# A new table of order, engines and banks for the same 2788 pieces of work, in an attention and gated-MLP kernel on one core

## The chip, the cores and the metric

One core of a Trainium2 chip runs the whole program. The metric is device time in microseconds (us) of one execution. TensorE is PE in the rows (its weight loads PEld), VectorE DVE, ScalarE ACT, GpSimd POOL. SyncE (SP) issues the transfers.

## What is computed

Attention with a multiplicative decay, then a gated projection. For each of 8 batches and 8 heads, with 576 positions and 64 dimensions a head:

```python
scores = q @ k.T / sqrt(64) + (cum[:, None] - cum[None, :])   # cum = cumsum(log(clip(f, 1e-4, 1)))
attn   = softmax(causal(scores)) ; attn_out = attn @ v
x      = attn_out with the heads side by side                  # (8, 576, 512)
gate   = sigmoid(causal depthwise conv of 5 taps over x)
out    = (gate * (x @ w_val)) @ w_out                           # float32
```

## The kernel before

**Pieces.** The two heads of a batch that share 128 partitions are a *pair*; there are 32. The kernel never writes its instructions in program order. It first records 2788 pieces of work (`Plan.add`, `Plan.dma`, lines 139 to 165), each with the buffers that it reads and writes, the engines that could run it, and the PSUM banks that it is the first to touch. Then it walks a table.

- *Loads* (`load_pair`, `load_rest`, lines 306 to 322): the pair's q and k go into `Xr[i % 2]`, its values into `vt[i % 2]`. The decay rows go into `dm[...]` and `dl[i % 2]` by broadcast from a DRAM tensor `decd`, which the kernel makes itself at the start.
- *Splits* (`plan_t`): from pair 4 on, `Xr` is split into a rounded part `Xh` (line 278) and a rest `Xl` (line 392), so that three fast matmuls replace a float32 one. Pairs 0 to 3 use `Xr` as it is.
- *Scores* (`plan_s`, lines 400 to 488): three PE groups a pair (line 263). For each of the 9 row blocks of a pair DVE adds the decay and takes the row minimum of the scaled negative (line 474), and ACT takes the exponential into `P` or `Pl` (line 478). A decay block is masked in place before its next, smaller use (`sel`), on POOL (line 483) or DVE (line 485). Pairs 0 and 1 take their decays from PE (`gate,gate` in the rows) and a fixed mask.
- *Transposes* (`plan_pt`): P is transposed by PE (lines 514, 532, 533) and copied from PSUM to `pt`, `pl` (line 278), on ACT or DVE. The reciprocals of the row sums ride along. They are written to DRAM (`rzd<-pl`) and read back by broadcast (`x<-rzd`).
- *Values* (`plan_pv`): P times V on PE, times the reciprocal (line 581), split into `xh`, `xl` (lines 278, 588). The convolution is five passes over `gate` (lines 283, 285, 623), then tanh (line 594).
- *MLP* (`plan_moe`): for each batch, the product with w_val (16 half groups, `Mv`), times the gate (line 655), split into `hh`, `hl` (line 669), and the product with w_out (`Mo`). Odd and even batches share output tiles. Results go by `ot` (lines 696, 698) to DRAM.
- *Weights* (`plan_w`): each quarter of the two weights is loaded into `ot` or `wu` and taken apart by seven short passes (lines 712 to 749).
- *Warming groups* (`warm`, line 358): six groups of four transposes of the identity, whose results nobody reads.

**What sets the order.** `TABLE` (line 46) is a string. Each entry names a piece (two digits in base 64), an engine (one digit: PE, ACT, DVE, POOL, SP) and, for each bank that the piece is the first to touch, the bank. The kernel issues the pieces in the table's order, so the table alone fixes every engine's queue. An engine takes its instructions in that order. A piece that waits holds up everything behind it on its engine, on SP too.

```python
while at < len(table):
    n, e = DIGITS.index(table[at]) * 64 + DIGITS.index(table[at + 1]), ENGINES[int(table[at + 2])]
    nd = self.nodes[n]
    at += 3
    assert nd["deps"] <= seen and e in nd["engs"]
    for k in nd["take"]:
        self.home[k] = range(int(table[at]), int(table[at]) + self.width[k])
        at += 1
    seen.update((n, done.get(n, n)))
    yield nd["fn"], e
```

Of the kernel before, what the change touches and what calls it, by code (L numbers as in the profile page):

```python
# [51 lines left out]
4p24t14z23B003N41o24v33I17k44q13z075k44E34w24x14F24G13o23m23p24A13R45V044L033A13W011p33C13U025z31s13r11t23P44B31B44C24D15W28K41u23s24K24M13q31v27x14X0
708I44T034e43X25X15w35s45v064513V27m44Y24Z41w17y34_47z17w31x21y25I0204U14V031A33t25A25x25F35511z11E20o078C44P073-
15C35G23Y15B15_041D15y15M34Q14N065D25E17A21F24O14W15J35144R075347_055N27C34S158035K25L156075S38R13u21G25P35T27o45Q29U45H13v25O11H18E4802a045928P38Q35R
15U15725Y281167028S28O3ba46017F33Z23_26813w16107690136a16b41I26219h059i26d47B002347G27D27I27J26j14037L35a19j163015Z078G47H10l055c36h46f45-
164165067M24126617K17P37E185057O0277Q29-47S37T26m018X37V37R14227U1a717Y3bg4a837W27N17u47X18U35b27Z29Y48627-
19W46k0687038816n28304a516l28226o11J284189008a15d2bi46p38T057328f0618g18j48h48b048p18c18Y28V29136w005e28-
38n48W18d068e19226x09l019315f28_26z058l48Z11M45g29839m1a62a43901953940469926A01L39626q16r21X49b39719e3az019c2aa36s2bc48s078t29a18q039d16t39f2dl4431bm3
aA29r048r29n07bp19g16P06aB11O19s26u29o16B29t049u19k26y2bn11R2ad39v039w1be46C16D36Q01K1a9047218M49x0539y16H006I09z49H1bo2ab2ae2ac1af1ag31P2bv2dr4ah2ai1
aj36E056F0bq3ak26J21Q26G2aq31S1an3al1am0431T2aD07ao2at39B4ar29p05aw3bR011U25h16K26L3aE11V1as16M001W2ap19q1dt4ax2ay1bS2bT19F4bs36N0dx2dy3aJ05aK26v1au2a  # L60
v16O2dz39D46R29I07dp49J26S16T3br03152bt21Z1bE006dA1bw2bu1by3eD42029K07bB3bx1dn4aH03aI1bV04bz28w39L2aL01bW1bC2aM16X036Y0bF38x2bG2bA1aC26U056V0bI3bJ2bO3
bH11-2eJ4eL4bL2bM2a24bD1dB3bK16Z2bP2aP014aQ1aT4bN1dD3bQ16W2aR4dG21_26-
28y2aN02aO1aZ1eH4aF07aG16_3e004e127006211222232e21aV4dC03017dE2dJ3dF1dH2dP052241dM3aX4dI1252eQ1dK2a-
04eS3b003dN2dT3fV4bU2dU2e400b12eF49M1eY3a_2dL1bk4710e51721g14734dQ29O1eR3c300dR2c41c5034cf1b42c61c74dW3dS18u17a01g81c94dZ37b08z2bX06b228A2b52bZ00dX2b6
# [763 lines left out]
```

## Time and profile before

| | us |
|---|---|
| three runs | 513.71, 515.65, 515.92 (median 515.65) |
| the profiled execution | 514.39 |
| its span, first to last instruction | 512.7 |
| PE busy | 498.9 (97%) |
| DVE busy | 434.4 (85%) |
| ACT busy | 359.8 (70%) |
| POOL busy | 230.0 (45%) |

The profiled execution lies 1.26 us under the median, and 1.7 us of it lie outside the span. PE is busy nearly throughout. What a new order can change is the time in which PE waits, so the rows to look for are PE's idle time by stretch, who ended it, and how full the engines are that feed PE in each stretch. The granted clock is 1.00 in all stretches, the higher of its two levels (2.4 GHz).

### The profile page before, as it was taken

The page shows a single profiled execution, that of the slowest core. Times are in us where ns is not written, and L with a number is a line of the kernel's source. Part 1 is how long each engine was busy: PE and PEld are TensorE (multiplying, and loading weights), DVE is VectorE, ACT ScalarE, POOL GpSimd, SP SyncE. Part 2 cuts the span into 40 slices and gives each one's busy share as a digit, 9 for nine tenths or more (in the row PEclk, how much of TensorE's full clock was granted, in tenths as well). Part 3 has the DMA queues.
Part 4 walks back from the last instruction along what each step waited for, and adds up shares of the span by engine and source line. Part 5 has one row for each costly group of instructions (what it writes and reads, how often), then busy time and mean ns, then how long its engine had stood idle before and what let it go on. Part 6 is the DMA issues. An engine that isn't in the chain of part 4 may idle for free.

```text
span 512.7 us, 12687 instructions
## 1 busy us (share of the span) xinstructions
PE 498.9 (97%) x4392; PEld 442.9 (86%) x4392; DVE 434.4 (85%) x1171; ACT 359.8 (70%) x973; POOL 230.0 (45%) x345
## 2 busy tenths in 40 slices
PE   6899899999999999999999999999999999999997
PEld 4677798988998889988999888899899888999985
DVE  6999999998988897899988988988988888977660
ACT  4999998885866765768777677787877766473122
POOL 3348785745644443347544635434742623201200
PEclk9999999999999999999999999999999999999999
DMA  7977564555563465446517364554665153122012
GB/s 264 270 232 251 174 164 158 150 164 181 169 213 102 138 182 174 153 143 195 172 58 254 104 215 129 192 183 143 203 201 176 58 156 106 45 74 68 21 63 102
DMA packets 35009, 79.49 MB, mean 155 GB/s; under 512 B 5057, under 2 KB 5313, under 8 KB 34945
## 3 DMA queue, kind: packets, MB, share of 16 engines
q1 hardware_dynamic: 34864, 78.54, 48.8%
q8 instruction: 34, 0.56, 0.5%
q14 instruction: 31, 0.25, 0.2%
q10 hardware_dynamic: 80, 0.15, 0.1%
HBM read 68.93 MB, written 9.73 MB: 153 GB/s over the span
## 4 chain that ended last, share of the span: by engine, by line
PE 77%; ACT 6%; DMA 6%; DVE 5%; issue 3%; SPq 2%; POOL 1%; DVEq 0%; ACTq 0%; POOLq 0%
PE banks L263 62%; PE banks L514 12%; ACT P L478 3%; DMA Xr<-in_x_dram 3%; PE banks L532 2%; SPq L289 2%; DVE gate L623 1%; ACT pt L278 1%; DVE banks L474 1%; DMA ot<-in_w_val_dram 1%; DMA x<-rzd 1%; PE banks L533 1%; DMA dl<-decd 1%; DMA dm<-decd 1%; ACT Xh L278 0%
## 5 line engine op out<-in xcount | busy, mean ns | idle before, releaser
L478 ACT ACTIVATE P<-banks,negm 128x512 f32<-128x512 f32 (+3 forms) x256 | 135.0, 535 | 35.2 <-DVE negm L474 33.2
L483 POOL TENSOR_SCALAR_AFFINE_SELECT dm<-dm 128x128 f32<-128x128 f32 x182 | 74.7, 420 | 122.8 <-DVE negm L474 113.0
L474 DVE CUSTOM_DVE_ANT_0 banks<-banks,dm 128x512 f32<-128x512 f32 (+3 forms) x240 | 115.1, 504 | 14.6 <-POOL dm L483 4.7
L278 ACT COPY pt<-banks 128x512 f32<-128x512 f32 (+1 forms) x185 | 93.8, 542 | 37.2 <-PE banks L514 32.2
L263 PE MATMUL banks<-xh,wall 128*128 128x288 f32 x512 | 113.4, 300 | 0.1
L623 DVE SCALAR_TENSOR_TENSOR gate<-x,cw,gate 128x576 f32<-128x576 f32 x126 | 110.2, 881 | 3.4 <-POOL gate L285 2.3
L263 PE MATMUL banks<-pt,vt 128*64 128x128 f32 (+1 forms) x1280 | 92.8, 297 | 0.4 <-DVE pt L278 0.2
L514 PE MATMUL banks<-ident,P 128*128 128x128 f32 x640 | 89.6, 277 | 2.3 <-ACT P L478 1.8
L263 PE MATMUL banks<-wall,hh 128*128 128x512 f32 x288 | 91.5, 399 | 0.0
L263 PEld LDWEIGHTS banks<-xh,wall 128*128 128x128 f32 x512 | 85.0, 188 | 1.0 <-DVE h L655 0.3
L263 PEld LDWEIGHTS banks<-pt,vt 128*64 128x64 f32 x1280 | 75.5, 137 | 8.5 <-issue 2.5
L514 PEld LDWEIGHTS banks<-ident,P 128*128 128x128 f32 x640 | 71.4, 140 | 12.3 <-ACT P L478 3.1
L263 PE MATMUL banks<-xl,wall 128*128 128x288 f32 x256 | 75.4, 295 | 0.0
L392 POOL TENSOR_TENSOR Xl<-Xr,Xh 128x640 fp32r<-128x640 f32 (+1 forms) x37 | 57.6, 1559 | 28.7 <-ACT Xh L278 12.1
L263 PEld LDWEIGHTS banks<-wall,hh 128*128 128x128 f32 x288 | 51.5, 188 | 9.0
L263 PE MATMUL banks<-Xh 128*128 128x288 f32 (+4 forms) x280 | 56.8, 335 | 0.9 <-DVE pt L278 0.5
L263 PE MATMUL banks<-wall,hl 128*128 128x512 f32 x144 | 56.5, 392 | 0.0
L478 ACT ACTIVATION_READ_ACCUMULATOR P<-banks,negm 128x1 f32 x256 | 53.2, 208 | 0.0
L263 PE MATMUL banks<-Xh,Xl 128*128 128x288 f32 (+4 forms) x280 | 53.1, 315 | 0.0
L263 PE MATMUL banks<-Xl,Xh 128*128 128x288 f32 (+4 forms) x280 | 53.0, 314 | 0.0
L263 PEld LDWEIGHTS banks<-xl,wall 128*128 128x128 f32 x256 | 48.2, 188 | 0.3
L263 PEld LDWEIGHTS banks<-Xh 64*128 64x128 f32 (+1 forms) x280 | 32.0, 185 | 10.0 <-issue 4.2
(104 smaller groups left out, 754.3 us busy)
## 6 DMA issues: line engine op xcount, KB each, us to landing
Xr<-in_x_dram SPq DMA_DIRECT2D x32, 608.0 KB
dm<-decd SPq DMA_DIRECT2D x60, 256.0 KB
vt<-in_v_dram SPq DMA_DIRECT2D x32, 320.0 KB
x<-rzd SPq DMA_DIRECT2D x64, 144.0 KB
out_dram<-ot SPq DMA_DIRECT2D x36, 256.0 KB
dl<-decd SPq DMA_DIRECT2D x60, 144.0 KB
ot<-in_w_val_dram SPq DMA_DIRECT2D x2, 512.0 KB
wu<-in_w_val_dram SPq DMA_DIRECT2D x2, 512.0 KB
```

What stands on the lines that cost most here:

```text
L263: nc.tensor.matmul(out, lhsT=lhsT, rhs=rhs, start=start, stop=stop)
L278: (eng.copy if eng is nc.scalar else eng.tensor_copy)(out=out, in_=in_)
L289: lambda e: (nc.sync if e == "SP" else nc.scalar).dma_start(out=out, in_=in_), reads, writes, **kw)
L392: eng.tensor_tensor(out=Xl[r][:, a:e], in0=Xr[r][:, a:e], in1=Xh[r][:, a:e].bitcast(F32), op=ALU.subtract)
L474: nc.vector.tensor_tensor_reduce(out=sl, in0=sl, in1=add, op0=ALU.add, op1=ALU.min, scale=-0.125, scalar=3.0e38, accum_out=negm[r][:, col])
L478: nc.scalar.activation(out=dst[:, o:o + ext], in_=bank(key)[:, c0:c0 + ext], func=AF.Exp, bias=negm[r][:, col], scale=-1.0, accum_out=zs[r ...
L483: eng.affine_select(out=t, in_=t, pattern=[[-1, P]], base=0, channel_multiplier=1, compare_op=ALU.is_ge, fill=-BIG)
L514: nc.tensor.transpose(out=bank(key)[:, c:c + P], in_=Pt[m][:, BOFF[b] + P * j:BOFF[b] + P * j + P], identity=ident)
L532: nc.tensor.transpose(out=bank(key)[:, P * j:P * j + P], in_=Pl[r][:, P * j:P * j + P], identity=ident)
L533: nc.tensor.transpose(out=bank(key4)[0:D + NN, 0:P], in_=Pl[r][:, L0:], identity=ident)
L623: eng.scalar_tensor_tensor(out=gt, in0=src, scalar=wt_, in1=gt, op0=ALU.mult, op1=ALU.add)
```

## The change

The string `TABLE` is replaced. It names the same 2788 pieces. Nothing else in the file changes; the new string is 4 lines shorter, so that line 263 before is line 259 now, and so on. The first lines of both:

```diff
 TABLE = """
-0240930b20520010e20z40B10740430n010E20a30p020C20630f10K40V40D20F10h20G20H20q030I20J228002450i20d30c30N22640M10P20Q12W40g12a00O22j0672f20R22g10j42h22i1
-0S20T12U42k22q22o22p12900U32d22l10u32e12s032t02m22b20Y20r30t32u24845m40X10-
...
+0010930430240z40740b20d20e20a30p010m000B10K40o020C20n030c30f10632U40520E20F10D20h20V40G228005310H20g10I20J20i20M10j40N20P20O22W40Q12a02h22i14642j0640R
+20S22o24a40T12m24c42902s012t00x30U31445o42f25k42p12n14442D072g12F032b22c12k24842q20Y20r32d22l10v32B000y32E10X15m40t32u22C12G20-
...
```

Nearly every place in every queue differs. Pieces that several engines can run are shared out anew, by these counts:

| piece | before: ACT, DVE, POOL | now: ACT, DVE, POOL |
|---|---|---|
| masking of `dm` (lines 483, 485) | -, 58, 182 | -, 56, 184 |
| masking of `dl` (line 320) | -, 12, 18 | -, 7, 23 |
| `Xh` (line 278) | 32, 8, 16 | 34, 4, 18 |
| `Xl` (line 392) | -, 19, 37 | -, 21, 35 |
| `xh` (line 278) | 24, 8, - | 21, 11, - |
| `xl` (line 588) | -, 17, 15 | -, 14, 18 |
| first pass of the convolution (lines 283, 285) | 13, 3, 16 | 14, 5, 13 |
| later passes (line 623; POOL lines 285, 621) | -, 126, 2 | -, 127, 1 |
| copies of transposes (line 278) | 207, 49, - | 206, 50, - |
| `hh` (line 278), `hl` (line 669) | 21, 26, 17 | 19, 27, 18 |
| output copies (lines 696, 698) | 31, 5, - | 28, 8, - |
| last weight passes (lines 278, 749) | 6, 5, 5 | 6, 3, 7 |

Three places, as the built programs have them.

**SP, near the start.** The names end in a buffer number: `Xr0` here is the load for pair 2, the third of all `Xr` loads; `Xr1` that for pair 1. Before:

```order
L289 DMA wu_125<-in_w_val_dram 128x1024
L289 DMA vt0_90<-in_v_dram 128x640
L289 DMA vt1_91<-in_v_dram 128x640
L289 DMA decd_68<-gate0_112 64x576
L289 DMA Xr1_76<-in_x_dram 128x1216
L289 DMA dm1_70<-decd_68 128x512
L289 DMA dm3_72<-decd_68 128x512
L289 DMA ot_123<-in_w_val_dram 128x1024
L289 DMA dl0_73<-decd_68 64x576 x2
L289 DMA dm0_69<-decd_68 128x512
L289 DMA dl1_74<-decd_68 64x576 x2
L289 DMA Xr0_75<-in_x_dram 128x1216
```

and now:

```order
L285 DMA ot_123<-in_w_val_dram 128x1024
L285 DMA Xr1_76<-in_x_dram 128x1216
L285 DMA wu_125<-in_w_val_dram 128x1024
L285 DMA decd_68<-gate0_112 64x576
L285 DMA vt1_91<-in_v_dram 128x640
L285 DMA dm0_69<-decd_68 128x512
L285 DMA dl0_73<-decd_68 64x576 x2
L285 DMA ot_123<-in_w_val_dram 128x1024
L285 DMA dl1_74<-decd_68 64x576
L285 DMA dm2_71<-decd_68 128x512
L285 DMA Xr0_75<-in_x_dram 128x1216
```

One load of `vt`, one of `dm` and one of `dl` that stood ahead of the load for pair 2 now stand behind it, and between the second load of `ot` and it there are two transfers instead of five.

**ACT, before its first exponential** (line 478 before, 474 now). Before:

```order
L720 ACTIVATE h32_114<-h32_114,ebias_126 128x20
L712 ACTIVATE gate1_113<-ot_123 128x512
L720 ACTIVATE ot_123<-ot_123,ebias_126 128x512
L351 ACT_TABLE_LOAD
L478 ACTIVATE P0_81,zs0_94<-banks_127,negm0_92 128x384
L478 ACTIVATE P1_82,zs0_94<-banks_127,negm0_92 128x384
```

and now:

```order
L716 ACTIVATE h32_114<-h32_114,ebias_126 128x20
L347 ACT_TABLE_LOAD
L708 ACTIVATE gate1_113<-ot_123 128x512
L716 ACTIVATE ot_123<-ot_123,ebias_126 128x512
L474 ACTIVATE P1_82,zs0_94<-banks_127,negm0_92 128x384
L274 CAST wall_124<-gate1_113 128x512
```

The load of the function table moved ahead of the two weight passes, which wait for the first weight (`ot`).

**PE, around the first matmuls of pair 2** (`banks<-Xr0`). The transposes have `ident`, line 360 is a warming group. Before:

```order
L263 MATMUL banks_127<-gate0_112,gate1_113 128x288 x2
L514 MATMUL banks_127<-ident_64,P1_82 128x128 x4
L263 MATMUL banks_127<-Xr0_75 128x288 x2
L514 MATMUL banks_127<-ident_64,P1_82 128x128 x2
L514 MATMUL banks_127<-ident_64,P2_83 128x128 x4
L360 MATMUL banks_127<-ident_64 128x128 x4
L514 MATMUL banks_127<-ident_64,P2_83 128x128 x4
```

and now:

```order
L259 MATMUL banks_127<-gate0_112,gate1_113 128x288 x2
L510 MATMUL banks_127<-ident_64,P2_83 128x128 x4
L510 MATMUL banks_127<-ident_64,P1_82 128x128 x4
L510 MATMUL banks_127<-ident_64,P2_83 128x128 x4
L510 MATMUL banks_127<-ident_64,P0_81 128x128 x4
L259 MATMUL banks_127<-Xr0_75 128x288 x2
```

Pair 2 now begins behind four transpose groups instead of one. The warming group is gone from here: four of the six now stand ahead of the first scores (16 transposes, three groups and 12 before), two later (three before).

## Rows read from the trace of the kernel before

**Rows 1.** The page, part 1: busy us, share of the span, instructions.

```profile
PE 498.9 (97%) x4392; PEld 442.9 (86%) x4392; DVE 434.4 (85%) x1171; ACT 359.8 (70%) x973; POOL 230.0 (45%) x345
```

**Rows 2.** Busy time by stretch: start:end, length, then engines; last clock, DMA share, GB/s.

```profile
0.00:7.00 7.00, 2.82 (x12) 2.42 (x12) 3.35 (x8) 2.39 (x4) 3.61 (x17) 1.00 0.66 208
7.00:30.00 23.00, 21.56 (x132) 15.11 (x133) 20.85 (x69) 20.53 (x57) 5.67 (x17) 1.00 0.85 260
30.00:100.00 70.00, 66.94 (x663) 58.24 (x662) 67.40 (x193) 64.03 (x177) 52.51 (x70) 1.00 0.64 196
100.00:200.00 100.00, 99.81 (x899) 89.58 (x897) 86.58 (x226) 71.47 (x196) 49.36 (x71) 1.00 0.52 156
200.00:300.00 100.00, 99.61 (x930) 90.22 (x930) 90.29 (x249) 72.16 (x201) 49.11 (x70) 1.00 0.49 161
300.00:400.00 100.00, 99.62 (x918) 89.56 (x916) 88.59 (x244) 76.10 (x210) 46.74 (x68) 1.00 0.55 177
400.00:480.00 80.00, 79.41 (x708) 73.04 (x705) 63.62 (x158) 45.98 (x121) 21.75 (x33) 1.00 0.27 81
480.00:512.70 32.70, 29.12 (x147) 24.71 (x145) 13.71 (x29) 7.19 (x13) 1.22 (x1) 1.00 0.20 73
```

**Rows 3.** Who waited for whom, PE: us in total, times, longest.

```profile
PE banks L263 <- DMA Xr<-in_x_dram: 2.6, 2, 1.5
PE banks L514 <- ACT P L478: 1.8, 5, 0.6
PE banks L360 <- ACT Pl L478: 1.0, 1, 1.0
PE banks L263 <- ACT P L478: 0.6, 2, 0.4
```

**Rows 4.** Order of time, SP, 16 to 27 us: start, us, what.

```profile
16.71 0.53 SPq L289 DMA_DIRECT2D Xr<-in_x_dram  x1
```

**Rows 5.** Order of time, PE, 24.9 to 27.3 us: start, us, what, [idle before, releaser].

```profile
25.20 1.21 PE L263 MATMUL banks<-Xr 128*128 128x288 f32 x4 [1.02 <-DMA Xr<-in_x_dram]
```

**Rows 6.** Order of time, DVE, 24.4 to 26.6 us.

```profile
26.55 0.77 DVE L474 CUSTOM_DVE_ANT_0 banks<-banks,dl 128x576 f32<-128x576 f32 x1 [1.19 <-PE banks L263]
```

**Rows 7.** The page, part 6: transfers issued, count, KB of one.

```profile
dm<-decd SPq DMA_DIRECT2D x60, 256.0 KB
vt<-in_v_dram SPq DMA_DIRECT2D x32, 320.0 KB
...
dl<-decd SPq DMA_DIRECT2D x60, 144.0 KB
```

**Rows 8.** Order of time, ACT, 7.9 to 12.3 us.

```profile
8.33 0.68 ACT L712 ACTIVATE gate<-ot 128x512 f32<-128x512 uint32 x1 [2.54 <-DMA ot<-in_w_val_dram]
...
10.30 1.28 ACT L351 ACT_TABLE_LOAD   x1
11.59 0.58 ACT L478 ACTIVATE P<-banks,negm 128x384 f32<-128x384 f32 x1
```

**Rows 9.** Order of time, DVE, 9.9 to 10.7 us: the first row minimum's last step.

```profile
10.46 0.14 DVE L474 DVE_READ_ACCUMULATOR2_ANT negm<- 128x1 f32 x1
```

**Rows 10.** Order of time, PE, 43.9 to 57.4 us: two of three late warming groups.

```profile
44.13 0.60 PE L360 MATMUL banks<-ident 128*128 128x128 f32 x4
...
57.01 0.66 PE L360 MATMUL banks<-ident 128*128 128x128 f32 x4 [0.95 <-ACT Pl L478]
```

**Rows 11.** Groups by shape, DVE: count, busy us, mean ns, idle before.

```profile
L623 DVE SCALAR_TENSOR_TENSOR gate<-x,cw,gate 128x576 f32<-128x576 f32 x126 | 110.2, 881 | 3.4 <-POOL gate L285 2.3
...
L485 DVE TENSOR_TENSOR dm<-dm,tri 128x128 f32<-128x128 f32 x58 | 26.2, 452 | 1.5 <-DMA dm<-decd 0.6
```

**Rows 12.** Line 485, its instructions: ns min/median/max, first and last start.

```profile
L485 DVE TENSOR_TENSOR dm<-dm,tri x58: 230/292/1507, 57.4 to 451.1; 128x128 f32<-128x128 f32 x58
```

**Rows 13.** Order of time, ACT and then PE, 302 to 306 us.

```profile
302.45 0.73 ACT L278 CAST Xh<-Xr 128x640 fp32r<-128x640 f32 x1 [2.10 <-DMA Xr<-in_x_dram]
...
305.14 0.92 PE L514 MATMUL banks<-ident,P 128*128 128x128 f32 x6 [0.38 <-ACT P L478]
```

**Rows 14.** The chain that ended last, 460 to 513 us: start, us, what.

```profile
468.12 4.17 DMA x<-rzd
...
479.27 29.86 PE banks L263 x150
```

More of the change, by code (lines that the diff above doesn't have):

```diff
@@ L52 @@
[L52 to L64, printed above, removed]
@@ new lines @@
+b22A13k21c23x043y11e23z033A12P42R41d14H014I21i23J0601h11q43K14J14l31k23T11l13L41j24h054734m24j23N47s41m24r34s24u0127k45z34o34p25u34n13H062H004y33P44k1
+1n24v33n042I14t14z23I11p33R44w21B44B33o21o11t23l004E34x13D053m21s13p23q33E14e45V034A11v21w14C27m44F23W005W23U064G14q15s41u21x21y24D11A34K25X13r13X24P0
+53V24V024Q14W14X0344Y13s21z23t28I43-
+17q45v001574_47z15515I0648K44Z47A38C45x25C34R037x15A25y11E25F34S17w34T024U11D14L004M15347y25145D25J35B10l027o45G25H11G25K25L15M35N23u25P39U48O25Q25S35
+T23v28G47_028028E44N008P38Q356014O15725E158077u45U15R161058R15O1a046215_006015Y28S25925Z065-
@@ new lines @@
+62e4079Q29R2fV4dY1c100eJ4c21g817a04hb4b_05c01ec068v3bZ017b0b-1c74dO1fi00dZ3d-
+275037608y2b52734e51c94g148z27c18A2eV3d_1b62cg07cd4eP3g92ed1fj2dV1e32ci04772fk1g61g73cb4eU032509S2f5061cj2ch2ck1cm19M2eW2eX1eZ2cl3784f23e804e929N3dv4e
+_2f32f02f638B17f07f41f92e-
+17g0fa2fb1eg043eq1eh2fm00ee02fn1fX4f_4ff3g53ef1cv03fZ4f72fc3f81fg2jh4fh1f11cn2co2cs04ct07h1ek4ei4em4hq2fd2fe1hr3cw0cu2cx2hd4ge3gA04ga01207ho1gB2gn063g
+C1hh4jp4hp2fq04gf2fr1fl2gg1gb3cD05gc2cI04gh2gi2gd1gj1cE0fw02jn4cp2gk3gl2fu01go3gp2gm1eo4ea00eb2cJ0cT07gr3cy1cA00gq1gs2cB0gt1eN4fv1et01b72b82fx1hf4gx3g
@@ new lines @@
+EA00Iv4DA4FC1FQ07EL1FK2FL1FY01Ai2Aj2Ak2Ax05Ay0FP2As2At3DG2DE2DJ3JL4Cq3FZ2Az2Au06EO4Al1Hw2EB2Av0EM4EQ4DH1DI3z31FR1HS03EU1Aw2AA1HT2Hs00712Hu2HU1Hx2HC2HF
+056EV04HD2Hz3v74EX03Hv1Hy1HJ3HY07AB3HE1HA2ES4HK2G0020EW2HP3HG3HB1Ff4EY2FS01HZ1JY1FT1FU03HL1AF04AG0FV1Cu2IL3G12G24G44HH2HM3HN2AC00J-
+1HO1AD0IH3HQ2Ix4IF3HI1vc4HR1FW07AH2Cv2FX2I203I31AE2AI1J804J92IK01067G84JN4DK2Ga1IX023Ja1HV2F-
+04J_3F_1G64AN05IO3AO0JP4IM2IN1IR3IS2IY2AK04AL0IT1IP2IU2I001IV2I_3JR4I12J02J53L14AS06IZ2IW1EZ1I-
+1AJ2AP2J23J32J62J41L34K43HW01Gd07DL2DM2Gb05HX1AM2AQ2E_3I6012IQ1ID4Jc00Hl4I72I404Gc2Ge2Ig1Jk02Gf2B005AR3Gh1H-
@@ L122 @@
+W01LY052Gm1GQ2M61GN2JH2LZ2LQ03KE06Kw07LU02Il2Ir2Im3KF1KA06LM05Kx1LV2L-4LN2GR2M04KT07LX1M44LR1KB2M902M703KR05GS3GZ0Mj06H601GU0M24G-
+1M82H70Ma2Md3Mb2KK4KO4KM4KU2KS2KX1H102Me2Mf2MC07Mm03Mc3B84KV2KW2Mk0Mn0MD0H20GV1GW4Is1Mu04JI2G_4H81KY2KZ2Mo2K-
+2K_2Mz05Mr03Ms0Mv0Mg2MH00Mh2JJ2Ml2Mp2Mq2JK1Mw2Mt2Mx1My2L01ME2MA0MB2MF2MK01ML0MI0Mi1MG2MJ2MM2MN2MO2H31H94H44MU06MP02N200MQ0MR2MS4MV0MW2MX4MZ03M-
+0M_1N04N30N41N54N704N80N91Na4
 """
```

110 lines of the change are left out of this document (50 added, 60 removed).

## The prediction, made before the changed kernel was run

> **What bounds the kernel now.** I read the page's busy shares first, then busy time by stretch, then PE's waits, and last the order of time around the longest of them. PE is busy 97% of the span [rows 1]. The new table names the same matmuls, so it can win only time in which PE waits. By stretch [rows 2] that time is small and lies mostly early. PE is idle 4.18 us before 7.0 us, where it waits for the first tiles; 1.44 us from 7 to 30 us; 3.06 us from 30 to 100 us; 0.19, 0.39, 0.38 and 0.59 us in the four stretches to 480 us; and 3.58 us after, of which most is the copy and the store of the last output tile. What an order can reach is the middle: 1.44 + 3.06 + 1.55 = **6.05 us**. Some waiting may hide inside busy PE, since its ends are modelled, but no row prices that.
>
> The reader should see two regimes in [rows 2]. From 30 to 100 us DVE is busy 67.40 of 70 us and ACT 64.03 of 70: both run as tight as PE, so each delay in front of them reaches PE. From 100 us on DVE is 87 to 90% busy and ACT 71 to 76%: they have a lead, and PE waits only at single places. The waits agree [rows 3]: PE stood 1.8 + 1.0 + 0.6 = 3.4 us for exponentials of ACT and 2.6 us for the loads of the first tiles.
>
> **The change, part by part.** The sum is made against the profiled execution, 514.39 us, which is 1.26 us under the median of 515.65; the differences are then taken from the median.
>
> *(a) The load for pair 2.* Before, it was issued at 16.71 us [rows 4], and PE's first matmul on it began at 25.20 us after 1.02 us of idling for that load [rows 5]. DVE had 1.19 us without work right behind [rows 6], in a stretch in which DVE has none to spare. In the new SP order one `vt`, one `dm` and one `dl` transfer less stand ahead of it: 320 + 256 + 144 = 720 KB [rows 7], at the 260 GB/s of that stretch [rows 2] 2.8 us. The two transfers between the second `ot` load and it, instead of five, let it issue sooner as well. On PE four transpose groups instead of one precede its first use. The wait of 1.02 us has no reason left. As DVE limits here, I count DVE's gap: **-1.2 us**, between 0 (DVE only does other work sooner and waits later) and -1.2. Late next is the load for pair 3, which now stands behind the first `rzd` writes; PE meets it nine groups after pair 2's in the new order, so I price that at 0.
>
> *(b) The function table.* ACT loaded it at 10.30 us for 1.28 us and began its first exponential at 11.59 [rows 8]. The row minimum for that exponential was there at 10.46 + 0.14 = 10.60 us [rows 9], so ACT started 0.99 us late. In the new order the load sits ahead of the weight passes, where ACT idled 2.54 us for the first weight [rows 8]; that idling covers it, and without it the load would cost its 1.28 us again. In all ACT also loses small pieces to the others (3 `xh`, 3 output copies, 2 `hh`), which helps the same waits. They were 3.4 us in sum [rows 3], so the gain lies between 0 and -3.4; I take the late start, **-1.0 us**, the only part with a row of its own. The Trainium skill ("ScalarE: Activation LUTs", section "What ACT_TABLE_LOAD costs") adds a drain of about 1.4 us to each switch of table. The exponential right behind the load at 11.59 us shows no such drain, so the row decides; by the page's figure (b) would be about -2.4, an estimate that I do not use.
>
> *(c) Warming groups.* Three stood late before, now two. One took 0.44 us of PE's time (four transposes; it shows as 0.60 with its modelled end), another stood in a gap of 0.95 us and cost nothing [rows 10]. So 0 to -0.44; **-0.2 us**.
>
> *(d) Pieces that change engines.* Over the run DVE gets 3 `xh`, 3 output copies, 2 `Xl`, 2 first convolution passes and some smaller ones, and loses 7 maskings, 3 `xl`, 4 `Xh`, 2 weight products. Priced at the mean of their kinds this is +2 us for DVE, -4 for ACT, +4 for POOL. After 100 us nothing of it shows: DVE has 10% or more free [rows 2]. In the early stretch what matters is how much DVE must have done when PE reaches a given place. I summed each queue by its kinds' usual durations up to what PE needs there. With 70 us of PE work done, DVE must have done 69.6 us now against 67.7; with 101 us done, 94.6 against 96.9. That is +1.9 at one place and -2.3 at another. I take **-0.2 us**.
>
> *(e) Loads in mid-run.* Before, ACT stood 2.10 us at 302.45 for an `Xr` tile, and PE 0.38 us behind it [rows 13]. Between issue and the first engine that meets the tile, the three shortest distances were 0.0, 2.4 and 3.5 us of PE work; they are now 0.7, 3.1 and 6.3. All of PE's idle time from 100 to 480 us is 1.55 us. I take half, **-0.8 us**, with 0 and -1.55 as bounds for the gain and as much for new waits.
>
> *(f) New close places.* For each of the 596 PE groups I compared the PE work between it and the group whose result it needs, by way of DVE and ACT, with the durations of the steps between. Under 0.5 us to spare had 60 before, 69 now. Of PE's work from 100 to 200 us, 8 places became 21. Eight such places cost 0.19 us there before [rows 2], so 13 more cost **+0.3 us**; at the early stretch's price they would cost far more, which is the third case below.
>
> The end is unchanged: PE closes with the same kind of output groups, which ran 29.86 us without a break [rows 14]. Now the last `rzd` writes stand 6 us of PE work later, and the reads of pairs 30 and 31 follow each other on SP, each landing about 4.2 us after issue [rows 14]. The first matmul that needs them still has 17 us of PE work ahead of it, as before. So 0.
>
> Sum: -1.2 - 1.0 - 0.2 - 0.2 - 0.8 + 0.3 = -3.1 us: 511.3 on the profiled execution's own scale, **512.6 us** on the median's.
>
> **The rivals.**
>
> *No change that can be measured* (within 0.5%, 2.6 us, which is about what a measurement of this kernel can tell). The mechanism is POOL slowing DVE. DVE's masking takes 292 ns in the middle and 452 in the mean, up to 1507 [rows 11, 12], and the convolution pass 881 in the mean [rows 11]: both have two inputs in SBUF. If each us of POOL's work takes one from DVE, the extra POOL work counts where DVE limits: up to PE's 101st us POOL must do 57.7 us instead of 55.9. That gives +1.8, so -1.3 us: 514.3. The Trainium skill ("SBUF — State Buffer", section "Who interferes with whom") says that a DVE instruction with two SBUF inputs and a POOL instruction that reads SBUF block each other for a whole instruction. The spread in [rows 12] agrees; whether the blocking adds up one for one no row shows. For this case: (a) and (b) are one-time delays that a fuller DVE takes back. Against it: DVE's own share there falls by 2.3 us, and DVE's loss on maskings is (452 - 292) x 58 = 9.3 us for all of POOL's 230 us [rows 1, 11, 12].
>
> *Slower.* The tight regime lasts until 200 us instead of 100. The place is the first two MLP batches, where 21 groups have under 0.5 us to spare. From 30 to 100 us PE idles 3.06 / 70 = 4.4% [rows 2]; over 100 us more that is 4.4 us, less the 0.19 there now, +4.2. Of the gains only (a) stays, as (b) to (e) suppose a lead: +3.0, 518.6 us. It decides when DVE is over 95% busy past 100 us; it is 86.58 of 100 now [rows 2], which speaks against it. The new close places speak for it.
>
> *All waits gone.* The new order clears the whole middle: -6.05 us, 509.6. Against it stand the 69 close places.
>
> *The change does nothing*: nearly every place differs, so the profile's waits must move; I give this no chance of its own.
>
> **How the numbers follow.** Forecast 40%, all waits gone 6%, no measurable change 34%, slower 20%. The first two are faster by over 0.5%: 46%. Same 34%, slower 20%. The forecast's own range is 511 to 513. The range that should hold 8 in 10 goes from 509.6, the whole middle gone, to 518.6, the tight regime lengthened; worse and better cases lie outside.
>
> **What would show it.** (a): no idle time of PE or DVE on the third `Xr` load, and its issue before 16 us. (b): the table load before 8 us and the first exponential near 10.6 us. (d), (f): PE's idle time from 30 to 100 us under 2.5 us, and from 100 to 200 us under 0.5. (e): no ACT wait of 2 us for `Xr`. If DVE is over 95% busy between 100 and 200 us, or a new load stops PE for over 1 us, the forecast is wrong; if PE's idle time falls as forecast and the time does not, PE's busy time hid the rest.

## The result, and the profile after

The changed kernel takes 508.65 us (median of 6 runs, 506.38 to 510.01) against 515.78 us for the kernel before in the same comparison (6 runs, 513.71 to 518.09). The ratio is **0.9851, 95% interval 0.9812 to 0.9889**: 7.1 us faster by the medians (7.7 us by the ratio, which goes by the means), more than twice the 3.1 us that was forecast. The profiled execution took 506.67 us, 7.7 us less than the one before.

The page, part 1, of the changed kernel, beside [rows 1]:

```profile
PE 496.5 (98%) x4392; PEld 442.2 (88%) x4392; DVE 426.9 (85%) x1168; ACT 357.1 (71%) x967; POOL 232.9 (46%) x353
```

PE does the same 4392 matmuls and is busy 2.4 us less. DVE has three instructions less and is busy 7.5 us less. POOL does more than before.

Busy time by stretch, with the columns of [rows 2]:

```profile
0.00:7.00 7.00, 3.93 (x18) 3.58 (x20) 3.58 (x9) 3.58 (x5) 3.34 (x17) 1.00 0.66 215
7.00:30.00 23.00, 22.11 (x143) 14.79 (x140) 22.45 (x73) 21.09 (x59) 5.84 (x17) 1.00 0.88 280
30.00:100.00 70.00, 69.02 (x699) 60.64 (x699) 66.50 (x195) 67.14 (x184) 54.06 (x74) 1.00 0.67 201
100.00:200.00 100.00, 100.00 (x898) 90.31 (x893) 86.68 (x230) 71.23 (x192) 46.59 (x64) 1.00 0.53 162
200.00:300.00 100.00, 100.00 (x929) 91.28 (x928) 89.30 (x250) 75.13 (x214) 56.22 (x86) 1.00 0.56 172
300.00:400.00 100.00, 100.00 (x936) 90.92 (x935) 86.33 (x240) 75.77 (x213) 48.61 (x74) 1.00 0.50 151
400.00:480.00 80.00, 80.00 (x672) 71.99 (x671) 61.07 (x151) 38.30 (x98) 18.23 (x26) 1.00 0.29 92
```

From 7 to 30 us PE now idles 0.89 us (1.44 before), from 30 to 100 us 0.98 (3.06), and from 100 to 480 us not at all (1.55). DVE is 86 to 89% busy from 100 to 400 us, much as before (87 to 90%), so the tight stretch was not lengthened.

Who PE waited for, with the columns of [rows 3]:

```profile
PE banks L510 <- ACT P L474: 0.9, 2, 0.6
PE banks L259 <- DMA Xr<-in_x_dram: 0.4, 1, 0.4
PE banks L510 <- ACT pt L274: 0.3, 1, 0.3
PE banks L356 <- ACT Pl L474: 0.3, 1, 0.3
```

The places that the forecast named, in order of time, SP, ACT and PE; they answer to [rows 4, 8, 5]:

```profile
14.40 0.43 SPq L285 DMA_DIRECT2D Xr<-in_x_dram  x1
...
5.93 1.28 ACT L347 ACT_TABLE_LOAD   x1
...
10.28 0.58 ACT L474 ACTIVATE P<-banks,negm 128x384 f32<-128x384 f32 x1 [0.36 <-DVE negm L470]
...
25.46 1.14 PE L259 MATMUL banks<-Xr 128*128 128x288 f32 x4
```

All four look as forecast: the load for pair 2 is issued before 16 us, PE does not idle for it, the function table is loaded while ACT waits for its weight, and the first exponential starts at 10.28 us. The experiments on the old order show no gain from these alone.

**PE's loss.** Idle time does not show all the waiting. Two pairs of neighbouring rows of the kernel before, order of time, PE:

```profile
219.49 0.40 PE L263 MATMUL banks<-wall,hl 128*128 128x512 f32 x1
219.72 0.62 PE L263 MATMUL banks<-wall,hh 128*128 128x512 f32 x2
...
221.54 0.39 PE L263 MATMUL banks<-wall,hl 128*128 128x512 f32 x1
222.32 0.40 PE L263 MATMUL banks<-Xh 128*128 128x288 f32 x1 [0.39 <-ACT P L478]
```

After such a matmul the next one starts 0.23 us later (219.49 to 219.72). At 222.32 it started 0.78 us later. So PE lost 0.55 us where the row shows 0.39: the modelled end of the matmul covers 0.16 us of each wait. I therefore summed PE's loss from starts: for each group of matmuls (one piece) the time to the start of the next group, minus the median of its kind in the kernel before. The table at the end of the experiments gives these sums by PE's own work done. For the two kernels, before and now: 5.2 and 4.2 us in PE's first 10 us of work, 8.6 and 5.3 from 10 to 115 us, **6.0 and 2.6 from 115 to 480 us**, 3.6 and 3.6 in the end. The differences make up the 7.7 us of the two profiled executions: 1.0 + 3.3 + 3.4.

### The profile page after: what moved, and what is told of

Same layout as the page of the kernel before. It is cut to its first block, busy times and chain, and to the rows that moved or that the text cites. A ratio compares the mean times of both kernels' runs of the same rounds, so it can differ in the third digit from the quotient of the medians.

```text
span 504.9 us, 12689 instructions
## 1 busy us (share of the span) xinstructions
PE 496.5 (98%) x4392; PEld 442.2 (88%) x4392; DVE 426.9 (85%) x1168; ACT 357.1 (71%) x967; POOL 232.9 (46%) x353
## 4 chain that ended last, share of the span: by engine, by line
PE 89%; ACT 5%; DVE 4%; DMA 1%; issue 1%; SPq 0%; ACTq 0%; DVEq 0%
PE banks L259 72%; PE banks L510 13%; PE banks L528 3%; ACT P L474 2%; ACT pt L274 1%; DVE banks L470 1%; DMA ot<-in_w_val_dram 1%; ACT Pl L474 1%; PE banks L529 1%; DVE gate L718 0%; ACT gate L708 0%; DVE negm L470 0%; SPq L285 0%; DVE x L577 0%; DVE gate L710 0%
## 5 line engine op out<-in xcount | busy, mean ns | idle before, releaser
L474 ACT ACTIVATE P<-banks,negm 128x256 f32<-128x256 f32 (+3 forms) x256 | 134.7, 534 | 27.4 <-DVE negm L470 24.9
L479 POOL TENSOR_SCALAR_AFFINE_SELECT dm<-dm 128x128 f32<-128x128 f32 x184 | 75.9, 423 | 108.9 <-DVE negm L470 83.2
L470 DVE CUSTOM_DVE_ANT_0 banks<-banks,dm 128x512 f32<-128x512 f32 (+2 forms) x240 | 114.8, 506 | 10.2 <-POOL dm L479 4.0
L619 DVE SCALAR_TENSOR_TENSOR gate<-x,cw,gate 128x576 f32<-128x576 f32 x127 | 105.3, 840 | 1.0
L510 PE MATMUL banks<-ident,P 128*128 128x128 f32 x640 | 88.4, 277 | 1.2 <-ACT P L474 0.9
L388 POOL TENSOR_TENSOR Xl<-Xr,Xh 128x640 fp32r<-128x640 f32 (+1 forms) x35 | 55.8, 1595 | 24.1 <-ACT Xh L274 13.4
L577 DVE TENSOR_TENSOR x<-banks,x 128x192 f32<-128x192 f32 (+1 forms) x64 | 27.9, 451 | 16.0 <-PE banks L259 5.8
```

What stands on the lines that cost most here:

```text
L388: eng.tensor_tensor(out=Xl[r][:, a:e], in0=Xr[r][:, a:e], in1=Xh[r][:, a:e].bitcast(F32), op=ALU.subtract)
L470: nc.vector.tensor_tensor_reduce(out=sl, in0=sl, in1=add, op0=ALU.add, op1=ALU.min, scale=-0.125, scalar=3.0e38, accum_out=negm[r][:, col])
L474: nc.scalar.activation(out=dst[:, o:o + ext], in_=bank(key)[:, c0:c0 + ext], func=AF.Exp, bias=negm[r][:, col], scale=-1.0, accum_out=zs[r ...
L479: eng.affine_select(out=t, in_=t, pattern=[[-1, P]], base=0, channel_multiplier=1, compare_op=ALU.is_ge, fill=-BIG)
L510: nc.tensor.transpose(out=bank(key)[:, c:c + P], in_=Pt[m][:, BOFF[b] + P * j:BOFF[b] + P * j + P], identity=ident)
L577: nc.vector.tensor_tensor(out=o, in0=bank(key)[:, 0:qb - qa], in1=o, op=ALU.mult)
```

## The experiments

All ratios are to the kernel before, in the same comparison. Its runs spread widely (511.86 to 519.86 us in 35 runs), so intervals are some 0.2 to 0.4% to each side. The losses of single executions help where the ratios are too coarse.

**Where along the run.** Both tables name the same pieces, and after some hundred entries both have named nearly the same ones. So one order can be followed up to an entry and the other from there on.

```diff
-TABLE: 2788 entries in the old order
+TABLE: the first 115 (head20), 361 (head55) or 740 (head115) entries of the new table, then the others in the old order
+TABLE: the first 740 (tail115) or 1115 (tail181) entries of the old table, then the others in the new order
```

> The first 115 pieces in the new order (PE's first 20 us), the rest in the old order. Theory A (the 7.8 us that the two profiled executions differ by were won piece by piece along the whole run; summed by PE's progress 2.0 us of them lie in the first 25 us of PE's work): about -2.0 us, ratio 0.996. Theory B (the early waits of pairs 0 to 2 are the cause, since the early queues are tight and all else follows from them): most of the gain, -5 to -7 us, ratio 0.986 to 0.990. Theory C (a gain in the first pairs is taken back by the next tight queue): 0, ratio 1.000.

> The first 361 pieces in the new order (PE's first 55 us), the rest in the old order. PE's loss between 10 and 100 us of its work was 8.4 us in the kernel before, 8.1 in head20, 8.3 in load_only, 5.3 in head115 and in the changed kernel. If the gain of the head lies from 20 to 55 us: 5.3 to 6 us here, ratio 0.996 to 0.997; if it needs the whole tight stretch (a gain won earlier is taken back by DVE and ACT): 7.5 to 8.4, ratio 0.999.

> The first 740 pieces in the new order (PE's first 115 us), the rest in the old order. Theory A: about -4.2 us, ratio 0.992. Theory B: the whole gain, -7 us, ratio 0.986. Theory C (the gain lies in the middle, where the old order keeps its waits): within 1 us, ratio 0.998 to 1.002. The forecast's own sizes (load -1.2, function table -1.0, warming group -0.2, engines -0.2) would give -2.6 us, ratio 0.995.

> The first 740 pieces in the old order, the rest in the new order: the complement of the run before. Theory A: about -3.6 us, ratio 0.993, and the two runs together give the whole change. Theory B: 0, ratio 1.000. The forecast's own sizes (loads -0.8, close places +0.3) would give -0.5 us, ratio 0.999. PE's idle time from 120 to 480 us should be under 0.5 us by theory A, about 1.5 us by theory B.

> The first 1115 pieces in the old order (PE's first 181 us), the rest in the new order, without a change of banks at the cut. tail115 lost 3.4 us in a single place just behind its cut (PE groups from 120 to 129 us) and from there on ran like the changed kernel (6.1 us beyond the usual group times, against 9.6 before). Theory A: the loss at the cut was the cut's own; here about -3.4 us, ratio 0.993. Theory B (what counts is the head): 0, ratio 1.000.

Measured: head20 0.9988 (0.9964 to 1.0013), head55 1.0029 (1.0006 to 1.0052), head115 0.996 (0.9935 to 0.9986), tail115 0.9999 (0.9974 to 1.0024), tail181 1.0001 (0.9979 to 1.0023). Only head115 won time, 2.1 us. The others must be read with care, since a cut can make a wait of its own. Order of time, PE, just behind the cuts of head55 and of tail181:

```profile
57.05 0.91 PE L514 MATMUL banks<-ident,P 128*128 128x128 f32 x6 [2.21 <-ACT pt L278]
```

```profile
185.99 0.50 PE L263 MATMUL banks<-Xh 64*128 64x512 f32 x2 [2.80 <-ACT Pl L478]
```

Neither of the two kernels whose orders were joined has such a wait there. tail115 lost 3.4 us at its cut and tail181 4.1 us from 150 to 200 us; behind that tail115 ran like the changed kernel (2.5 us of loss from 115 us on, 2.6 in the changed one). A long hold also gives the other engines a lead, so these two don't prove theory A, and head55 and head20 (2.0 us lost in two places just behind its cut) don't settle where in the head the gain lies. head115 has no such place and keeps the head's gain: 5.9 us of loss from 10 to 115 us. Theory B falls, as the new head alone leaves two thirds of the gain unexplained.

**The forecast's steps, one at a time.** The old order with the load for pair 2 moved (SP):

```diff
-L289 DMA vt_90<-in_v_dram 128x640
 L289 DMA vt_91<-in_v_dram 128x640
...
-L289 DMA dm_72<-decd 128x512
...
-L289 DMA dl_74<-decd 64x576 x2
-L289 DMA Xr_75<-in_x_dram 128x1216
+L289 DMA dl_74<-decd 64x576
+L289 DMA Xr_75<-in_x_dram 128x1216
+L289 DMA vt_90<-in_v_dram 128x640
+L289 DMA dm_72<-decd 128x512
+L289 DMA dl_74<-decd 64x576
```

> The old order with one edit on SP: the load for pair 2 moved ahead of one load of vt, one of dm and one of dl. Theory A: the first tile lands sooner too, since the vt load no longer shares the first 7 us: PE's first score starts 0.4 us earlier and the 1.02 us of idling at the third Xr tile goes, -1.2 to -1.6 us, ratio 0.997. Theory C: the idling goes, but DVE and ACT meet the next wait, 0 to -0.5 us, ratio 0.999 to 1.000.

Measured: 1.0036 (1.0016 to 1.0056), slower by 1.9 us. Order of time in load_only: PE, then POOL, DVE and PE again.

```profile
2.64 2.82 PE L360 MATMUL banks<-ident 128*128 128x128 f32 x12 [2.64 <-POOL ident L326]
6.42 3.36 PE L263 MATMUL banks<-Xr 64*128 64x512 f32 x8 [0.96 <-DMA Xr<-in_x_dram]
...
28.10 0.60 POOL L320 TENSOR_TENSOR dl<-dl,tri 128x64 f32<-128x64 f32 x2 [5.95 <-DMA dl<-decd]
...
28.73 0.77 DVE L474 CUSTOM_DVE_ANT_0 banks<-banks,dl 128x576 f32<-128x576 f32 x1 [2.43 <-DMA Xr<-in_x_dram]
...
29.98 0.30 PE L533 MATMUL banks<-ident,Pl 128*73 128x128 f32 x1 [1.39 <-DVE Pl L493]
```

PE's 1.02 us of idling for the `Xr` tile is down to 0.13 us, and a wait of 1.39 us stands 5 us further on. In this execution the tile did not come sooner: SP issued the load at 17.25 us (16.71 before), as it stood longer in front of the second `ot` load (issued at 14.60 us, 13.38 before), and PE's first matmul on the tile began at 25.28 us (25.20 before). The idling shrank because PE came 1.0 us later, after slow first matmuls (3.36 us instead of 1.77; they come back below). The half of `dl` that moved back is pair 3's, and the old order masks pair 3's `dl` on POOL *before* pair 2's. So POOL stood 5.95 us for a late transfer with pair 2's ready masking behind it, then DVE 2.43 us, then PE. (DVE's row names `Xr`, but that tile was long in use; what came last was `dl`.) The new table masks pair 2's `dl` first: there the load and POOL's order go together. How much of the 1.9 us each of the two, the late `dl` and the slow start, cost is not shown: by the table below this execution lost 1.4 us more than the kernel before in PE's first 10 us of work and about the same from 10 to 115 us.

The old order with the function table moved (ACT):

```diff
+L351 ACT_TABLE_LOAD
 L712 ACTIVATE gate_113<-ot 128x512
 L720 ACTIVATE ot<-ot,ebias 128x512
-L351 ACT_TABLE_LOAD
```

> The old order with the load of the function table moved ahead of the weight passes on ACT. The forecast's term b: the first exponential starts about 1.0 us earlier, at 10.6 us, and the time falls by 1.0 us, ratio 0.998. Theory C (DVE, 100% busy from 10 to 25 us, takes the lead back): the first exponential moves, the time does not, ratio 1.000.

Measured: 0.9999 (0.9977 to 1.002). Order of time in table_only, ACT and PE:

```profile
5.64 1.28 ACT L351 ACT_TABLE_LOAD   x1
...
10.66 0.58 ACT L478 ACTIVATE P<-banks,negm 128x384 f32<-128x384 f32 x1 [0.35 <-DVE negm L474]
...
25.79 1.94 PE L263 MATMUL banks<-Xr 128*128 128x288 f32 x4 [1.85 <-DMA Xr<-in_x_dram]
```

The exponential starts 0.93 us earlier, at the time that the forecast gave, and PE then waits 1.85 us for the `Xr` tile instead of 1.02. Of these 0.83 us more, 0.24 are the lead that was left when PE came to the tile; the other 0.59 are the tile, which came later (25.79 us against 25.20) though its load was issued at the same time (16.73 us against 16.71). This is the slowest of the kernel's 12 executions (517.95 us). So theory C has the ratio on its side, and three quarters of the lead were gone 13 us later, but the interval (1.2 us faster to 1.0 us slower) does not exclude the 1.0 us that the forecast counted.

One late warming group moved to the front of the old order, and all three edits together:

```diff
-L360 MATMUL banks<-ident 128x128 x12
+L360 MATMUL banks<-ident 128x128 x16
```

> The old order with one edit on PE: one of its three late warming groups moved to the front, so that 16 identity transposes instead of 12 stand ahead of the first scores. Theory D (with 12 of them, executions occur in which TensorE runs its first matmuls at half rate: the first 8 score matmuls took 3.36 us in load_only, the first 6 took 2.72 in tail115, and 8 took 1.77 in the kernel before, in the changed one, in head20 and in head115, the last three with 16 transposes): 1.77 us for the first 8, and -0.5 to -2.0 us in the median, ratio 0.996 to 0.999, as only a part of the executions before is affected. Rival (the forecast's term c, a late group costs PE 0 to 0.44 us and an early one nothing): -0.2 us, ratio 1.000, with the lowest times unchanged.

> The old order with the three edits that the forecast priced at the start, together: the load for pair 2 ahead of one vt, one dm and one dl; the function table ahead of the weight passes; 16 early transposes instead of 12. The forecast's sizes give -1.2 - 1.0 - 0.2 = -2.4 us, ratio 0.995. Theory D alone (load_only was slow by 1.9 us because its first matmuls ran at half rate; the loads and the table themselves bring little, as head20 gained 0.6 us): -0.5 to -1 us, ratio 0.998 to 0.999. If load_only was slow because its later dm and dl came too late: +0.5 us or more, ratio over 1.001.

Measured: warm_only 0.9983 (0.9963 to 1.0003), load_table_warm 1.0034 (1.0014 to 1.0055). The first is a gain of 0.9 us or none, and the 1.77 us that theory D expected of it were missed in its profile: the first 8 matmuls ran at the slow rate there too (3.15 us to the start of the next group), behind 16 transposes. In the second the load for pair 2 is issued at 15.59 us, PE meets the tile at 23.70 us with 0.24 us of idling, and then waits 1.6 us for DVE's line 493 again, as in load_only. With the slow start all but gone (4.0 us of loss in PE's first 10 us of work) the time is as long as load_only's, which speaks for the late transfers as the cause but does not show it: the profiled execution (514.49 us) is near the fastest of its 12 (514.25 to 519.03).

The old order with the new table's engines:

```diff
-each piece on the engine of the old table
+each piece on the engine of the new table (314 of 2788 differ), in the old order
```

> The old order, each piece on the engine that the new table gives it (314 pieces change engine). The forecast's term d: -0.2 us, ratio 1.000. If engines and order only belong together: slower by 1 us or more, ratio over 1.002; if the gain lies in the engines: 0.990 to 0.995.

Measured: 1.0946 (1.0914 to 1.0978), 48.8 us slower. The choice of engines has no worth of its own here; it fits its own order.

**POOL beside DVE.** In the kernel before, PE's largest holds between 100 and 480 us are 0.36 us at 179, 0.53 at 220, 0.35 at 228, 0.54 at 304 and 0.64 us at 404. Order of time, DVE and POOL, just before three of them:

```profile
178.66 2.01 DVE L623 SCALAR_TENSOR_TENSOR gate<-x,cw,gate 128x576 f32<-128x576 f32 x1
178.63 1.43 POOL L588 TENSOR_TENSOR xl<-x,xh 128x576 fp32r<-128x576 f32 x1
...
217.23 2.91 DVE L623 SCALAR_TENSOR_TENSOR gate<-x,cw,gate 128x576 f32<-128x576 f32 x2
218.11 1.42 POOL L669 TENSOR_TENSOR hl<-h,hh 128x576 fp32r<-128x576 f32 x1 [1.48 <-ACT hh L278]
...
225.81 1.47 DVE L485 TENSOR_TENSOR dm<-dm,tri 128x128 f32<-128x128 f32 x1
225.72 1.41 POOL L392 TENSOR_TENSOR Xl<-Xr,Xh 128x576 fp32r<-128x576 f32 x1
```

Line 623 by its instructions, ns min/median/max, with the columns of [rows 12]:

```profile
L623 DVE SCALAR_TENSOR_TENSOR gate<-x,cw,gate x126: 760/815/2065, 38.6 to 487.0; 128x576 f32<-128x576 f32 x126
```

A convolution pass that takes 815 ns in the median took 2.01 us, and a masking of 292 ns took 1.47. Each began beside a subtraction on POOL and ended shortly after it (0.61 us after for the pass, 0.15 for the masking): DVE stood still for most of POOL's instruction. Behind each on DVE was the pass that PE needed next. At 404 us it was a masking of 1.14 us beside `hl`.

In the next two kernels POOL's subtractions read one column and then only write (what is left out is the rest of each subtraction):

```diff
+    def rest(eng, out, x, xh):
+        w = 1 if eng is nc.gpsimd else out.shape[1]
+        eng.tensor_tensor(out=out[:, 0:w], in0=x[:, 0:w], in1=xh[:, 0:w].bitcast(F32), op=ALU.subtract)
+        if w == 1:
+            for _ in range(2):
+                eng.memset(out[:, 1:].bitcast(F32), 0.0)
...
-        any_("xl", {"POOL": 1.4, "DVE": 0.67}, p, lambda eng: eng.tensor_tensor(
-            out=xl[s], in0=xv, in1=xh[s][:, :].bitcast(F32), op=ALU.subtract), [*xk, ("xh", s)], [("xl", s)])
+        any_("xl", {"POOL": 1.4, "DVE": 0.67}, p, lambda eng: rest(eng, xl[s], xv, xh[s][:, :]), [*xk, ("xh", s)], [("xl", s)])
...
```

> The old order, with POOL's 69 subtractions of the rests (Xl, xl, hl) cut to their first column and followed by two fills with zero, which read nothing in SBUF and take about as long; DVE keeps its own subtractions whole. The part that is left out: the rests made on POOL. Theory P (in the middle PE waits because a DVE pass with two SBUF inputs stands still beside a POOL subtraction: at 178.66 us a convolution pass took 2.01 us beside one of 1.43, at 225.81 a masking took 1.47 beside one of 1.41): the convolution passes' mean falls from 881 to about 815 ns, DVE's maskings from 452 to about 290, and the time by 2 to 4 us, ratio 0.992 to 0.996. Rival L (late loads and close places make the waits): DVE's means fall, the time by under 1 us, ratio over 0.998.

> The new order with the same edit (71 subtractions on POOL). Theory P: the new order already keeps most of these pairs apart (its convolution passes take 840 ns in the mean, its maskings 379), so little is left to win: 0 to -1 us beside the changed kernel's 0.985, so the distance between the two kernels shrinks from 7 to 4 us or less. Rival L: both kernels move alike and the distance stays.

Measured: **before_fill 0.9916 (0.9888 to 0.9944), changed_fill 0.9858 (0.9826 to 0.989)**. The old order gained 4.3 us and the new one nothing, so that 3.6 us are left between them (511.44 and 507.85). DVE's passes, by line with ns min/median/max, first in the changed kernel, then in before_fill; [rows 11, 12] are the kernel before:

```profile
L619 DVE SCALAR_TENSOR_TENSOR gate<-x,cw,gate 128x576 f32<-128x576 f32 x127 | 105.3, 840 | 1.0
L481 DVE TENSOR_TENSOR dm<-dm,tri 128x128 f32<-128x128 f32 x56 | 21.0, 379 | 0.7
L481 DVE TENSOR_TENSOR dm<-dm,tri x56: 230/291/1520, 57.6 to 449.8; 128x128 f32<-128x128 f32 x56
```

```profile
L629 DVE SCALAR_TENSOR_TENSOR gate<-x,cw,gate 128x576 f32<-128x576 f32 x126 | 102.9, 823 | 3.2 <-POOL gate L292 2.2
L492 DVE TENSOR_TENSOR dm<-dm,tri 128x128 f32<-128x128 f32 x58 | 18.2, 314 | 1.7 <-DMA dm<-decd 0.9
```

The means were 881 and 452 ns before. So in the new order DVE stands still for (881 - 840) x 126 + (452 - 379) x 58 = 9.4 us less, while POOL's busy time rose from 230.0 to 232.9 us. Maskings over 0.5 us fell from 15 to 5. In before_fill the holds at 179, 220, 228, 304 and 404 us are gone, and PE's loss from 115 to 480 us is 2.8 us, the changed kernel's 2.6. Theory P holds. Standing alone does not set the price, though: in changed_fill the means fell on from 840 to 823 ns and from 379 to 312, about 6 us less standing, and the time stayed. What remained of it in the new order stood where PE did not wait for the next pass.

The edit is not pure, as it makes the rests ready sooner and POOL less busy. The page, part 1, of before_fill:

```profile
PE 498.9 (97%) x4392; PEld 443.6 (87%) x4392; DVE 419.0 (82%) x1171; ACT 360.1 (70%) x973; POOL 215.4 (42%) x497
```

POOL's 215.4 us stand against 230.0 before. So its 4.3 us are not the price of the standing alone, and I tried the cause with all of the work done: the old order with four small moves (DVE first, POOL from line 392 on).

```diff
-L623 SCALAR_TENSOR_TENSOR gate_112<-x_96,cw,gate_112 128x576
 L278 COPY pt_87<-banks 128x256
+L623 SCALAR_TENSOR_TENSOR gate_112<-x_96,cw,gate_112 128x576
...
-L623 SCALAR_TENSOR_TENSOR gate_113<-x_97,cw,gate_113 128x576 x2
+L623 SCALAR_TENSOR_TENSOR gate_113<-x_97,cw,gate_113 128x576
 L474 ISA banks,negm_93<-banks,dm_72 128x512
...
+L623 SCALAR_TENSOR_TENSOR gate_113<-x_97,cw,gate_113 128x576
...
-L485 TENSOR_TENSOR dm_70<-dm_70,tri_66 128x128
...
-L392 TENSOR_TENSOR Xl_80<-Xr_76,Xh_78 128x576
-L278 CAST Xh_78<-Xr_76 128x640
+L278 CAST Xh_78<-Xr_76 128x640
+L392 TENSOR_TENSOR Xl_80<-Xr_76,Xh_78 128x576
...
+L483 AFFINE_SELECT dm_70<-dm_70 128x128
 L278 CAST Xh_77<-Xr_75 128x640
 L669 TENSOR_TENSOR hl_120<-h_114,hh_116 128x64
```

> The old order with all of its work and four edits, one at each place where PE waits behind a DVE pass beside a POOL subtraction: two convolution passes moved behind the DVE pass that PE needs next (178.7 and 218.1 us), one subtraction on POOL moved behind its neighbour (225.7), one masking moved from DVE to POOL (403.3). Theory P: these four holds cost 0.36 + 0.53 + 0.35 + 0.64 us, so -1.9 us, ratio 0.996, and PE's loss from 100 to 480 us of its work falls from 6.2 to about 4.3 us. Rival (another pair collides instead): ratio 0.999 to 1.001 and the loss stays near 6.

Measured: 0.997 (0.995 to 0.9991), 1.5 us faster where 1.9 were expected; the loss from 115 to 480 us is 4.4 us. Order of time in four_apart, DVE and POOL, at the second place:

```profile
218.93 0.69 DVE L474 CUSTOM_DVE_ANT_0 banks<-banks,dm 128x512 f32<-128x512 f32 x1
...
219.54 0.73 DVE L474 CUSTOM_DVE_ANT_0 banks<-banks,dm 128x512 f32<-128x512 f32 x1
...
219.07 1.42 POOL L669 TENSOR_TENSOR hl<-h,hh 128x576 fp32r<-128x576 f32 x1 [1.47 <-ACT hh L278]
```

The same subtraction now lies beside two DVE passes that read one operand from PSUM. They take their usual 0.7 us, and PE does not wait there. The moves also made a new collision of the same kind. Order of time in four_apart, POOL, DVE and PE:

```profile
239.34 1.67 POOL L392 TENSOR_TENSOR Xl<-Xr,Xh 128x640 fp32r<-128x640 f32 x1
239.50 2.12 DVE L623 SCALAR_TENSOR_TENSOR gate<-x,cw,gate 128x576 f32<-128x576 f32 x1
...
243.47 0.33 PE L263 MATMUL banks<-pt,vt 128*64 128x128 f32 x2 [0.39 <-ACT Pl L478]
```

DVE's next pass for PE (line 474) starts at 241.75 us instead of 241.17, and PE loses 0.63 us at 243 us, where the kernel before has no such hold. By itself this would make the gain smaller than the expected 1.9 us; other waits shifted too, so the sum does not come out to the tenth.

**Do the parts add up?** The head in the new order, the rest in the old one, with the edit of before_fill:

> The first 115 us in the new order, the rest in the old, and POOL's subtractions of the rests cut to one column and followed by two fills with zero, as in before_fill (the rests made on POOL are left out). Theory P + head (the change is two parts that add: 0.9916 for the pairs kept apart, 0.996 for the head): 0.9876, and with the profiles' own sums (3.3 and 3.1 us) 0.9875, beside the changed kernel's 0.985. Rival (the two are one cause, seen twice): no better than before_fill, 0.992.

Measured: 0.9856 (0.9826 to 0.9887), the ratio of the changed kernel. The two parts add, within the noise: -2.1 and -4.3 us make -6.4, and -7.4 were measured, which the intervals allow. Against the changed kernel nothing of size is left over.

**The first matmuls.** The new order with 12 and with 20 early transposes instead of 16:

> The new order with one edit on PE: the fourth early warming group moved behind pair 4, so that 12 transposes stand ahead of the first scores. Theory D: the first 8 score matmuls take up to 3.4 us in some executions, +0.5 to +2.5 us beside the changed kernel's 0.985, so ratio 0.986 to 0.990. Rival (the number of early transposes does not matter): 0.985.

> The new order with one of its two late warming groups moved to the front, 20 early transposes instead of 16. Theory D: TensorE has no idle time left before its first scores, so no execution starts at half rate: -0.5 to -1 us beside the changed kernel, ratio 0.983 to 0.984, and the highest times of its range go. Rival (the transposes themselves now delay the first scores): +0.2 to +0.5 us, ratio 0.986.

Measured: 0.9882 (0.9858 to 0.9907) with 12, 0.9851 with 16, **0.9841 (0.981 to 0.9872)** with 20. The last is the fastest version, 507.42 us (507.18 to 508.60), but its interval and that of the changed kernel overlap, so it is not shown to be faster; nor is the kernel with 12 shown to be slower. Order of time, PE, the first scores, with 12 (the row holds four matmuls) and with 20 (eight):

```profile
7.58 2.08 PE L259 MATMUL banks<-Xr 64*128 64x512 f32 x4 [2.11 <-DMA Xr<-in_x_dram]
```

```profile
7.10 2.37 PE L259 MATMUL banks<-Xr 64*128 64x512 f32 x8
```

PE's loss in its first 10 us of work is 6.4 us in the mean of the eight profiles with 12 early transposes (4.9 to 8.5), 4.6 in the eight with 16 (4.0 to 5.9) and 4.0 in the one with 20. That more early transposes help has this on its side; the timed intervals of warm_only and of changed_12_early allow 0 to 2 us. But theory D as it was put, that without idle time no execution starts at half rate, missed: with 20 PE did not idle before its first scores, and still the first two matmuls took 1.01 us to the start of the next two, as with 12 (0.53 us in the kernel before); the next two took 0.54 us (0.42 in the kernel before), and from the fifth on they ran at the full rate.

PE's loss by its own work done, us, from one profiled execution each (engines_only left out):

| kernel | ratio | 0-10 | 10-115 | 115-480 |
|---|---|---|---|---|
| before | 1 | 5.2 | 8.6 | 6.0 |
| changed | 0.9851 | 4.2 | 5.3 | 2.6 |
| head20 / head55 | 0.9988 / 1.0029 | 4.1 / 4.2 | 8.3 / 10.3 | 7.6 / 6.9 |
| head115 | 0.996 | 5.0 | 5.9 | 5.2 |
| tail115 / tail181 | 0.9999 / 1.0001 | 6.0 / 6.2 | 11.5 / 6.6 | 2.5 / 5.7 |
| load_only / table_only | 1.0036 / 0.9999 | 6.6 / 4.9 | 8.5 / 11.0 | 6.8 / 7.5 |
| warm_only / load_table_warm | 0.9983 / 1.0034 | 5.9 / 4.0 | 8.5 / 9.2 | 6.2 / 6.7 |
| before_fill / changed_fill | 0.9916 / 0.9858 | 8.5 / 4.7 | 8.0 / 5.4 | 2.8 / 2.3 |
| four_apart | 0.997 | 6.3 | 8.6 | 4.4 |
| head115_fill | 0.9856 | 4.4 | 6.9 | 2.7 |
| changed_12_early / changed_20_early | 0.9882 / 0.9841 | 7.7 / 4.0 | 4.3 / 6.2 | 2.4 / 2.4 |

The last column follows the order that its stretch has, whatever was done ahead of it: 5.2 to 7.6 us in the old order, 2.3 to 2.8 in the new one or with POOL's reads gone, and four_apart between them (tail181 changes its order at 181 us). The first two columns belong together, since a late start can hide a later wait: tail181 runs the old head unchanged, lost 1.0 us more than the kernel before in the first column, and has no wait for the third `Xr` tile in the second. In their sum the old order up to 115 us, with the small edits or without, lies at 12.8 to 16.5 us and the new one at 9.5 to 11.3 (12.0 in changed_12_early). tail181 and the kernel before, alike up to there, differ by 1.0 us in the sum and 2.0 in the second column; so much is chance between single executions.

## Why the prediction was wrong

The sign was right, and the forecast case, faster by more than 0.5%, is the one that came. The size was wrong: 7.1 us instead of 3.1, past the case in which all of PE's waits in the middle go (-6.05 us), which was thought to be the limit.

- **The step that failed is (e), the middle of the run, and the case that was built on POOL.** (e) took PE's idle time from 100 to 480 us, 1.55 us, for all that could be won there, and put it down to late `Xr` loads; with (f) it came to -0.5 us. The loss from 115 to 480 us of PE's work was 6.0 us and fell by 3.4. Four of the five largest holds came from DVE passes beside POOL's subtractions. The fifth, the wait for `Xr` [rows 13], went as well when POOL's reads were cut; whether the transfer had waited for POOL was not tried by itself.
- **Blocking was priced by POOL's total work.** The forecast saw the spread of the masking [rows 12], charged the blocking at +1.8 us for 1.8 us more work on POOL, as a reason for no gain, and put nothing of it in the sum. It depends on which DVE pass stands beside which POOL instruction. POOL's work grew, the standing fell, and this was about half of the gain or more: 3.4 us by PE's loss in the middle, 4.3 us (2.9 to 5.8) by before_fill, which also spares POOL work. The weighing (452 - 292) x 58 = 9.3 us was in the text, but was set against all of POOL's time and not against PE's single holds.
- **"No row prices" the waiting inside busy PE** was too quick. The starts of neighbouring rows price it, 0.16 us a wait. PE's busy time fell by the 2.4 us that idle time did not show.
- **(a) and (b), -2.2 us: rows right, gain wrong.** Every sign named for them came true in the changed kernel, and in the old order they were worth +1.9 us (with the harm done to `dl`) and 0 (within about 1 us either way); with (c) beside them, +1.8 us. In place of the wait that went, PE met another. The forecast gave 0 as the bound of (a) for this reason and then took the other end.
- **(c), -0.2 us:** the late group was priced and the early one was not. The fourth early group may be worth up to 2 us at the start; the intervals do not show it.
- **(d), -0.2 us:** engines alone cost 48.8 us. A sum over engines of an order that does not exist says nothing.
- The sum of (a) to (d), -2.6 us, is near the 2.1 us of head115, but by luck, as none of its parts was seen to earn its share, alone or (a) to (c) together. What in the order of the first 115 us earns it stays open: the cuts at 20 and 55 us made waits of their own. The banks were not tried by themselves; every kernel with the new order has its banks too.
- **The slower case** needed DVE over 95% busy past 100 us; it is 86.7% from 100 to 200 us. That reading was right.

## What to carry to other kernels

Look for single instructions that take two or three times the median of their kind on an engine that feeds the bound engine, and see what ran beside them; where such a place holds the bound engine up, put an instruction with another source of operands there before shortening anything. A wait that can be named is worth at most what the next wait leaves of it, so look one wait further in the same queues before pricing it. And measure an engine's loss from start to start, as idle time leaves out a part of every short wait.
